# Attention and a mixture of experts on one core: x of the last two experts turned by DMA transposes of 16-bit planes, their routings let go earlier, and 34 idle matmuls for 12 behind the first gather

## The chip, the core and the metric

The kernel runs on one core of one Trainium2 chip. The core has five engines with queues of their own: TensorE (PE in the profile; its weight loads stand as PEld), VectorE (DVE), ScalarE (ACT), GpSimd (POOL) and SyncE (SP), which here only issues DMAs. The metric is the device time of one execution in microseconds (us), as the median of several. Profiles come from one profiled execution; their times count from the start of its span. L855 means line 855 of the kernel.

## What is computed

Attention with capped scores over 8 batches of 12 heads, 448 positions and 64 dimensions, and behind it a mixture of 8 experts, in float32:

```
scores = cap*tanh(q k^T/(8*cap));  attn = softmax(scores);  x = attn v      # x: 3584 tokens x 768
logits = x @ w_gate                                                        # 3584 x 8
# all 28672 logits in falling order: a token goes to an expert if it has none yet
# and the expert has fewer than cap = 3584/8 = 448 tokens
for e in range(8):
    h = relu(x[mask_e] @ w1[e])          # 448 x 768 @ 768 x 1024
    out[mask_e] = h @ w2[e]              # 448 x 1024 @ 1024 x 768
```

## The kernel before

The attention fills the first 335 us or so. Its last part, and the search that fills the first expert (routing 0), end at about 370 us. From there PE runs the experts one behind the other, in the order in which they filled; p counts them from 0 to 7.

**An expert.** Its 448 tokens' rows are fetched from the DRAM tensor xs by four indirect DMAs of POOL (`gather`, L782: rows 0-127, 128-255, 256-383, 384-447 of the expert, group j=0 to 3) into the tile xg. As the first product needs x with its 768 dimensions across partitions, x is turned: `xtr` (L798) turns one chunk c of 128 dimensions with four PE transposes, and `cutx` (L803, L804) reads them from PSUM and cuts them into a high part in PE's short float format and a low rest (xgh, xgl). Weights come in pieces by SP (`load1`, `load2`: w1r in four buffers, w2r in four) and are cut in the same way by ACT (L755) and POOL (L759) in `split1` and `split2`. `ffn1` computes h in 8 steps f of 18 matmuls of 448 columns (6 chunks times high-high, high-low, low-high): 144 matmuls. `ffn2` computes the output in 8 tiles u, of 24, 24, 24 and 16 matmuls of 384 columns, twice: 176 matmuls. Their results lie in psH, which has three buffers in PSUM; ACT evacuates each (L833 in ffn1, L861 and L864 in ffn2), with DVE behind it in ffn1 (L835). POOL scatters the output rows (L840).

**The order of the work.** For PE, ACT, DVE and POOL the program's order is the order of issue (manual_schedule); SP's order in this part is left to a planner. One matmul of ffn1 or ffn2 is one tick; an expert has 320. `tick` issues other work at set ticks: the next step of the routing generator, scatters, and the next expert's gather as soon as its tokens are known (L810). The routing of expert p+1 runs beside expert p: a search of three selections (not for the last expert), then `finalise`, which writes the expert's number (`ei`, L609) and token list (`idx`, L648). A hold in `phases0` (L678) lets finalise go at tick 145 of expert p's 320, the first of ffn2, for p+1 from 2 on. The turning of x for expert p+1 lies in tiles u=5, 6 and 7 of expert p's ffn2 (the table CP); two pieces of its weights are cut at u=5 and u=6. SP's loads for expert p+1 wait for ei and for free buffers.

**The start of the experts.** Behind routing 0 three pieces of w1 are loaded, the first gather is issued, and 12 idle matmuls (`warm(NW)`, L711; each stands in the profile as two records) keep PE at work. Then the steps of the next routing follow, whose first PE work (L477) waits for DVE, then `tx`, which turns four chunks as the four groups land, with four idle matmuls between two groups, and then the first matmul of ffn1. Further loads wait for the third group of the gather, by a copy of one value of it (tok).

Of the kernel before, what the change touches and what calls it, by code (L numbers as in the profile page):

```python
# [323 lines left out]


YL=[]
ACF=1
LF=1
TA=0
# [2 lines left out]
class Routing:  # L332
# [266 lines left out]
    def finalise(s,wp,L,update):  # L599
# [8 lines left out]
        ei=wp.tile([1,1],I32,name="ei",bufs=8)  # L608
        v.tensor_scalar(ei,s.e8s[0:1],-1.0,8.0,op0=ALU.mult,op1=ALU.add)  # L609
        s.ei=ei  # L610
        yield 8 if s.cur==1 else 12
        ps=s.psum()
        warm=(lambda n: s.warm(n)) if s.cur==0 else (lambda n: None)
        nc.tensor.matmul(ps[:112,0:2],s.lo,sc[:,:,NC-1],start=True,stop=False)
# [19 lines left out]
        ps=s.psum()  # L634
# [8 lines left out]
        ps=s.psum()  # L643
# [5 lines left out]
        s.results.append((idx,s.ei))  # L649
        yield 1  # L650
        if update:
          with s.tc.issue_after(mark.ins) if s.cur==0 else nullcontext():
            z=wp.tile([112,1],F32,name="zz")
            v.tensor_scalar(z,oi[:,0,0,0:1],0.0,None,op0=ALU.mult)
# [14 lines left out]
    def phases0(s,wp,L,turned):  # L669
        HA=[7,10]; HB=3  # L670
        for p in range(s.E):
            s.hA=HA[min(p,len(HA))-1] if p else 7; s.hB=HB; s.na=2 if p<9 else 1
            s.cur=p
            if p:
                s.propose(L,0,s.NC)
                yield 30
            yield from (s.search(wp,turned if p==0 else ()) if p<s.E-1 else s.last(wp))
            yield -((p-1)*320+145) if p>1 else 4  # L678
            yield from s.finalise(wp,L,p<s.E-1)


W1B=4; W2B=4
def ffn_all(nc, tc, ctx, rt, xs, w1, w2, out, ident, E, wp, deferred, xctx, gen):
# [11 lines left out]
    def units(n):  # L695
        for _ in range(n):
            if deferred: late.append(deferred.pop(0)())
    def posts():
        while late: late.pop(0)()
    N0=1; UN=[1,2,1,2,0,2,2,1,2,2,0,2,2,2,0,0]  # L700
    ctx.enter_context(tc.manual_schedule(engines={ET.PE,ET.Activation,ET.DVE,ET.Pool}))
    with tc.issue_after(rt.mark[0].ins):
        units(1)
    posts()
    m=0
    wu=[None]; end=[-99]
# [22 lines left out]
    def need(p):  # L729
        while len(res)<=p: step()  # L730
    ereg={}
    def expert(p):
        need(p)
        if p not in ereg: ereg[p]=nc.sync.value_load(res[p][1][0:1,0:1],min_val=0,max_val=E-1)
        return ereg[p]
    raw={}; spl={}; lp=[False]; tt=[False]
    gap=f2.tile([1,1],F32,name="gap")
    def load1(p,i,gate=None):
        if p>=E: return
        e=expert(p)  # L740
        t=ws.tile([128,DC,128],F32,name="w1r",bufs=W1B)
        if gate is not None: nc.gpsimd.tensor_copy(t[0:1,0,0:1],gate)
        nc.sync.dma_start(t,w1[bass.ds(e,1),:,i*128:i*128+128].rearrange("o (c p) f -> p (o c) f",p=128))
        raw[p,1,i]=t
# [31 lines left out]
    nc.gpsimd.memset(xgp[64:128,3*DM:],0.0)  # L776
    def gather(p):
        if p>=E or p in xgs: return
        need(p)
        t=xgs[p]=xgp  # L780
        for j,(o,n) in enumerate(TS):
            g=nc.gpsimd.indirect_dma_start(out=t[:n,j*DM:(j+1)*DM],out_offset=None,in_=xs,in_offset=bass.IndirectOffsetOnAxis(ap=res[p][0][:n,j:j+1],axis=0))  # L782
        return g
    def tx(p,n):
        newx(p)
        w=rt.psum()
        ps=[(ph.tile([128,512],F32,name="psH") if c>1 else pt.tile([128,512],F32,name="psX")) for c in range(n)]
        for j,(o,_) in enumerate(TS):
            for c in range(n): nc.tensor.transpose(ps[c][:,o:o+128],xgs[p][:,j*DM+c*128:j*DM+c*128+128],ident)
            if j<len(TS)-1: warm(WJ,w)  # L790
        for c in range(n): cutx(p,c,ps[c])
    def xtr(p,c):
        if p>=E or c is None: return
        newx(p)
        gather(p)
        ps=pt.tile([128,512],F32,name="psX")
        for j,(o,n) in enumerate(TS):
            nc.tensor.transpose(ps[:,o:o+128],xgs[p][:,j*DM+c*128:j*DM+c*128+128],ident)  # L798
        cutx(p,c,ps)
    def cutx(p,c,ps):  # L800
        h,l=xgT[p]
        src=ps[:,:C]
        nc.scalar.activation(h[:,c,:],src,AF.Copy)  # L803
        lo=nc.vector.tensor_tensor(l[:,c,:],src,h[:,c,:].bitcast(F32),op=ALU.subtract)  # L804
    pend=[]; cnt=[0]; cur=[0]; bc=[0]; BG=11
    def tick(n=1):
        cnt[0]+=n; bc[0]+=n; now[0]+=n
        if bc[0]>=BG:
            if pend: bc[0]=0; scatter(*pend.pop(0))
        if len(res)>cur[0]+1 and cur[0]+1 not in xgs: bc[0]=0; gather(cur[0]+1)  # L810
        if cnt[0]>=hint[0]:
            cnt[0]=0; step()
    hh={}
# [62 lines left out]
    step(); step()  # L876
    step()
# [5 lines left out]
    for p in range(E):  # L883
# [34 lines left out]

def full(nc,tc,q,k,v,cap,wg,w1,w2,out):
    with ExitStack() as ctx:  # L920
# [26 lines left out]
        ffn_all(nc,tc,ctx,r,xs,w1,w2,out,ident,8,wp,deferred,xctx,r.phases(wp,L1,turned))  # L947


_INS=["q","k","v","cap","moe_w_gate","moe_w1","moe_w2"]  # L950
# [24 lines left out]
```

## Time and profile before

| | us |
|---|---|
| median of 3 runs | 906.33 |
| lowest, highest | 905.64, 906.44 |
| the profiled execution | 906.85 |
| its span | 905.1 |

The 1.75 us between the profiled execution's time and its span lie outside of the instructions. The page of the profile lists the busy time of the engines. Views of the trace used below are the order of time of one engine (start, duration, engine, line, operation, tiles, count; in brackets the idle time before it and what ended it), groups of instructions by line, the stretches of time with the busy time and count of each engine, and the DMA issues with their time to landing.

### The profile page before, as it was taken

The numbers are of one execution on the slowest core, as the hardware profiler recorded it, in microseconds if no ns is written. First come the engines' busy times: TensorE is split into PE (matmuls) and PEld (weight loads), VectorE is DVE, ScalarE is ACT, GpSimd is POOL, SyncE is SP. The second block draws the span as 40 slices with busy tenths as digits, with TensorE's granted clock in tenths as the row PEclk, the third lists the DMA queues.
The fourth block names the chain that finished last, engine by engine and source line by source line (L and its number), as shares of the span: only waits on it lengthen the run. The fifth ranks groups of instructions, "written<-read, shape, count | busy, mean of one in ns | idle before, by whom it ended". The sixth has DMA issues, their size and how long they took to land.

```text
span 905.1 us, 17559 instructions
## 1 busy us (share of the span) xinstructions
PE 876.5 (97%) x6320; PEld 643.3 (71%) x6320; DVE 604.0 (67%) x2004; ACT 564.0 (62%) x844; POOL 349.9 (39%) x501
## 2 busy tenths in 40 slices
PE   6899999999999997799999999999999999999997
PEld 3333444444333345789989989989999999999997
DVE  3688988989888888766776776767767764231210
ACT  6998898889899948273582672762752752532521
POOL 8100000000000009482593492592682773754841
PEclk9999999999999999999999999999999999999999
DMA  8799999997994017741915616407407407416301
GB/s 117 113 136 140 128 171 173 139 164 120 198 175 72 1 58 246 248 157 45 313 45 171 196 36 226 157 19 236 150 18 253 149 3 251 149 55 236 112 10 53
DMA packets 291704, 123.09 MB, mean 136 GB/s; under 512 B 224768, under 2 KB 275712, under 8 KB 291104
## 3 DMA queue, kind: packets, MB, share of 16 engines
q1 hardware_dynamic: 285104, 99.70, 49.9%
q0 software_dynamic: 4656, 22.02, 6.8%
q8 instruction: 50, 0.82, 0.4%
q10 hardware_dynamic: 1856, 0.23, 0.2%
q14 instruction: 38, 0.31, 0.1%
HBM read 97.15 MB, written 24.77 MB: 135 GB/s over the span
## 4 chain that ended last, share of the span: by engine, by line
PE 72%; issue 12%; POOL 5%; DVE 5%; SPq 3%; DMA 1%; ACT 1%; POOLq 0%; ACTq 0%; DVEq 0%
PE psH L827 20%; PE psH L855 18%; PE psA L189 12%; PE psS L148 10%; PE psM L206 4%; SPq L92 2%; PE psS L153 2%; POOL w1l L759 2%; PE psX L798 2%; PE psM L37 1%; POOL out_dram L840 1%; POOL w2l L759 1%; DVE es L165 1%; POOL xg L782 1%; DVE cmpD L503 1%
## 5 line engine op out<-in xcount | busy, mean ns | idle before, releaser
L855 PE MATMUL psH<-w2h,hh 128*128 128x384 f32 x896 | 247.0, 342 | 0.0
L855 PE MATMUL psH<-w2l,hh 128*128 128x384 f32 x512 | 175.0, 342 | 0.0
L154 ACT ACTIVATE e<-psS 128x896 f32<-128x896 f32 x168 | 147.6, 909 | 31.3 <-PE psS L148 18.7
L855 PEld LDWEIGHTS psH<-w2h,hh 128*128 128x128 f32 x896 | 162.3, 189 | 0.2
L159 ACT ACTIVATE e<-e,bias 128x1792 f32<-128x1792 f32 (+2 forms) x74 | 147.3, 1991 | 2.0
L827 PE MATMUL psH<-xgh,w1h 128*128 128x448 f32 x384 | 143.4, 373 | 0.3 <-ACT xgh L803 0.3
L827 PE MATMUL psH<-xgh,w1l 128*128 128x448 f32 x384 | 141.6, 369 | 0.0
L827 PE MATMUL psH<-xgl,w1h 128*128 128x448 f32 x384 | 141.2, 368 | 0.0
L148 PE MATMUL psS<-tq,tk 64*64 64x448 f32 x1152 | 130.9, 548 | 7.4 <-DVE tq L133 3.4
L759 POOL TENSOR_TENSOR w1l<-w1r,w1h 128x768 fp32r<-128x768 f32 x62 | 114.2, 1843 | 28.6 <-ACT w1h L755 22.5
L189 PE MATMUL psA<-e,nv 64*64 64x448 f32 x1104 | 120.9, 541 | 1.2 <-DVE xT L199 1.2
L759 POOL TENSOR_TENSOR w2l<-w2r,w2h 128x768 fp32r<-128x768 f32 x64 | 118.1, 1846 | 9.0 <-ACT w2h L755 8.7
L459 POOL TENSOR_SCALAR r_Bt<-r_b 112x4 f16<-112x4 int32 x1 | 0.2, 199 | 303.7 <-DVE rin L243 303.7
L165 DVE TENSOR_TENSOR es<-es,e 64x896 f32<-64x896 f32 (+2 forms) x74 | 100.4, 1356 | 2.7 <-ACT e L159 1.3
L835 DVE SCALAR_TENSOR_TENSOR hh<-psH,hh 128x64 fp32r<-128x64 f32 (+1 forms) x128 | 44.1, 386 | 81.2 <-ACT hh L833 79.7
L861 ACT ACTIVATE on<-psH 128x384 f32<-128x384 f32 x48 | 23.6, 491 | 119.6 <-PE psH L855 119.6
L855 PEld LDWEIGHTS psH<-w2l,hh 128*128 128x128 f32 x512 | 96.5, 189 | 0.0
L148 PEld LDWEIGHTS psS<-tq,tk 64*64 64x64 f32 x1152 | 43.7, 133 | 73.9 <-issue 40.7
L189 PEld LDWEIGHTS psA<-e,nv 64*64 64x64 f32 x1104 | 46.5, 134 | 59.9 <-issue 50.5
L833 ACT ACTIVATE hh<-psH 128x448 fp32r<-128x448 f32 x64 | 34.8, 544 | 73.2 <-PE psH L827 61.1
L827 PEld LDWEIGHTS psH<-xgh,w1h 128*128 128x128 f32 x384 | 72.5, 189 | 5.9 <-ACT xgh L803 0.5
L827 PEld LDWEIGHTS psH<-xgh,w1l 128*128 128x128 f32 x384 | 72.3, 188 | 5.7
(334 smaller groups left out, 1320.6 us busy)
## 6 DMA issues: line engine op xcount, KB each, us to landing
w1r<-in_moe_w_dram SPq DMA_DIRECT2D x64, 384.0 KB, 3.9
w2r<-in_moe_w_dram SPq DMA_DIRECT2D x32, 768.0 KB, 8.0
k<-in_k_dram SPq DMA_DIRECT2D x92, 112.0 KB, 3.4
q<-in_q_dram SPq DMA_DIRECT2D x92, 112.0 KB, 4.0
nv<-in_v_dram SPq DMA_DIRECT2D x72, 128.0 KB, 3.9
xs<-xn SPq DMA_DIRECT2D x4, 1344.0 KB, 7.4
xs<-xn SPq DMA_DIRECT2D x4, 896.0 KB, 5.1
xd<-xT SPq DMA_DIRECT2D x2, 1344.0 KB, 7.0
```

The costliest lines, as they stand in the source:

```text
L148: for c in range(2): nc.tensor.matmul(ps[c*64:c*64+64,h,:S],tks[g,0][hp,o,u*128+c*64:u*128+c*64+64],tks[g,1][hp,o,:],start=True,stop=True)
L154: nc.scalar.activation(ev(g,r),ps[:,:,:S],AF.Tanh,scale=sr[0])
L159: act=lambda: nc.scalar.activation(e,e,AF.Exp,scale=sr[1],bias=bias)
L165: t=es_t[g]; add=lambda o,a,b: nc.vector.tensor_tensor(o,a,b,op=ALU.add)
L189: nc.tensor.matmul(avp[g,o][h*64:h*64+64,:S],lhs,rhs[hp,h,:],start=(j==0 and x==0),stop=j==3)
L206: nc.tensor.matmul(ps[g*32:g*32+32,:S],lhs,rhs,start=first,stop=last)
L759: (eng or nc.gpsimd).tensor_tensor(view(l),r,view(h).bitcast(F32),op=ALU.subtract)
L827: nc.tensor.matmul(ps[:,:C],a[:,c,:],b[:,c,:],start=(m==0),stop=(m==DC*3-1)); m+=1
L833: nc.scalar.activation(h[:,:C],ps[:,:C],AF.Relu)
L835: nc.vector.scalar_tensor_tensor(h[:,d:d+b-a],ps[:,a:b],0.0,h[:,a:b].bitcast(F32),op0=ALU.max,op1=ALU.subtract)
L855: nc.tensor.matmul(ps[:,:HD],h[:,f,a:a+128],spl[p,2,hf,f//2][w][:,f%2,:],start=(m==0),stop=(m==nm-1))
L861: if t<3: nc.scalar.activation(ons[p][0][:,t*DM+hf*HD:t*DM+hf*HD+HD],ps[:,:HD],AF.Copy)
```

## The change

For p from FT=6 on, PE no longer turns x. Instead, for each group j, ACT copies the gathered float32 rows, seen as 16-bit halves, into a tile pl with one plane of low and one of high halves, and its queue writes them to a DRAM tensor xz with the two planes of a token as neighbouring rows. When two groups are written, one DMA transpose of SP's queue turns 16-bit elements of [512, 768] or [384, 768] back into xg, where the two halves of a number come to lie side by side: x is turned, as float32. `cutt` then cuts it from SBUF, in four steps (two halves k of the tokens, three chunks each) at matmuls 8, 13, 18 and 23 of tile u=6. xg becomes two tiles, one for each k. `planes` of the groups follow the gather by 26, 36, 46 and 56 ticks.

For these two experts finalise is let go at tick 125 and 118 instead of 145 and waits 18 ticks instead of 12 for its first matmul; `early` issues the loads of three pieces of w1 and one of w2 as soon as ei is computed. SP's order is the program's from the start of the experts on, three blocks that asked the planner for an order are gone, and NW is 34 instead of 12.

```diff
+LK=(0,0,145,145,145,145,125,118); FT=6
...
+        if s.cur>=FT: s.early(s.cur,ei)
-        yield 8 if s.cur==1 else 12
+        yield 8 if s.cur==1 else 18 if s.cur>=FT else 12
...
-            yield -((p-1)*320+145) if p>1 else 4
+            yield -((p-1)*320+LK[p]) if p>1 else 4
...
-    ctx.enter_context(tc.manual_schedule(engines={ET.PE,ET.Activation,ET.DVE,ET.Pool}))
-    with tc.issue_after(rt.mark[0].ins):
-        units(1)
+    ctx.enter_context(tc.manual_schedule(engines={ET.PE,ET.Activation,ET.DVE,ET.Pool,ET.SP}))
+    units(1)
...
+    def early(p,ei):
+        ereg[p]=nc.sync.value_load(ei[0:1,0:1],min_val=0,max_val=E-1)
+        for i in range(3): load1(p,i)
+        load2(p,0)
+    rt.early=early
...
-    xgp=fp.tile([128,4*DM],F32,name="xg")
+    xgp=[fp.tile([128,2*DM],F32,name=f"xg{k}") for k in range(2)]
+    row=lambda j,n=128: xgp[j//2][:n,j%2*DM:(j%2+1)*DM]
...
+    TD=26; TJ=10; xq=[]
+    def planes(j):
+        o,n=TS[j]; k,r=divmod(j,2)
+        pl=fp.tile([128,2,DM],I16,name="pl",bufs=2)
+        nc.scalar.activation(pl[:n],row(j,n).bitcast(I16).rearrange("p (d h) -> p h d",h=2),AF.Copy)
+        nc.scalar.dma_start(xz[k][r*256:r*256+2*n].rearrange("(p h) d -> p h d",h=2),pl[:n])
+        if r:
+            n=o+n-2*128*k
+            nc.sync.dma_start_transpose(xgp[k][:,:DC*n].bitcast(I16).rearrange("p (c t) -> p c t",c=DC),xz[k])
+    def cutt(p,k,c0,c1):
+        newx(p)
+        o,n=((0,256),(256,192))[k]
+        h,l=(t[:,c0:c1,o:o+n] for t in xgT[p])
+        x=xgp[k][:,c0*n:c1*n].rearrange("p (c t) -> p c t",c=c1-c0)
+        nc.scalar.activation(h,x,AF.Copy)
+        nc.vector.tensor_tensor(l,x,h.bitcast(F32),op=ALU.subtract)
...
-        if len(res)>cur[0]+1 and cur[0]+1 not in xgs: bc[0]=0; gather(cur[0]+1)
+        if len(res)>cur[0]+1 and cur[0]+1 not in xgs:
+            bc[0]=0; n=cur[0]+1; gather(n)
+            if n>=FT:
+                xq.extend((now[0]+TD+TJ*j,lambda j=j: planes(j)) for j in range(4))
+        while xq and xq[0][0]<=now[0]: xq.pop(0)[1]()
...
-    WG=3; NW=12; WJ=4
+    WG=3; NW=34; WJ=4
     for i in range(WG): load1(0,i)
-    mk=gather(0)
-    with tc.issue_after(mk.ins):
-        tok=xgp[0:1,2*DM:2*DM+1]
-        for i in range(WG,W1B): load1(0,i,tok)
-        load2(0,0,tok)
-        load2(0,1,tok)
+    gather(0)
+    tok=xgp[1][0:1,0:1]
+    for i in range(WG,W1B): load1(0,i,tok)
+    load2(0,0,tok)
+    load2(0,1,tok)
     warm(NW)
...
-            if u==4: load1(p+1,0); load1(p+1,1)
-            if u==5: load1(p+1,2); load2(p+1,0)
+            if p+1<FT:
+                if u==4: load1(p+1,0); load1(p+1,1)
+                if u==5: load1(p+1,2); load2(p+1,0)
             if u==6: load1(p+1,3)
             if u==7: load2(p+1,1)
...
-            ffn2(p,u%4,u//4,(CL if p<1 else CP)[u],wk)
+            if p+1>=FT and not lastp:
+                for m,k,c in {6:[(8,0,0),(13,1,0),(18,0,3),(23,1,3)]}.get(u,()): wk[m]=wk.get(m,[])+[lambda k=k,c=c: cutt(p+1,k,c,c+3)]
+            ffn2(p,u%4,u//4,(CL if p<1 else CP)[u] if p+1<FT else [],wk)
...
+        xz=[dr.tile([n,768],I16,name=f"xz{i}") for i,n in enumerate((512,384))]
```

More of the change, by code (lines that the diff above doesn't have):

```diff
@@ L651, in finalise @@
         if update:
-          with s.tc.issue_after(mark.ins) if s.cur==0 else nullcontext():
+          if True:
             z=wp.tile([112,1],F32,name="zz")
@@ L677, in phases0, with ffn_all @@
             yield from (s.search(wp,turned if p==0 else ()) if p<s.E-1 else s.last(wp))
-            yield -((p-1)*320+145) if p>1 else 4
+            yield -((p-1)*320+LK[p]) if p>1 else 4
             yield from s.finalise(wp,L,p<s.E-1)
 W1B=4; W2B=4
-def ffn_all(nc, tc, ctx, rt, xs, w1, w2, out, ident, E, wp, deferred, xctx, gen):
+def ffn_all(nc, tc, ctx, rt, xs, xz, w1, w2, out, ident, E, wp, deferred, xctx, gen):
     C=448; DM=768; DC=6; DF=1024; FC=8; HD=384
@@ L732, in expert @@
     def expert(p):
+        if p in ereg: return ereg[p]
         need(p)
-        if p not in ereg: ereg[p]=nc.sync.value_load(res[p][1][0:1,0:1],min_val=0,max_val=E-1)
+        ereg[p]=nc.sync.value_load(res[p][1][0:1,0:1],min_val=0,max_val=E-1)
         return ereg[p]
@@ L774, in newx @@
         if p not in xgT: xgT[p]=(fp.tile([128,DC,C],F32R,name="xgh"),fp.tile([128,DC,C],F32R,name="xgl"))
-    xgp=fp.tile([128,4*DM],F32,name="xg")
-    nc.gpsimd.memset(xgp[64:128,3*DM:],0.0)
+    xgp=[fp.tile([128,2*DM],F32,name=f"xg{k}") for k in range(2)]
+    row=lambda j,n=128: xgp[j//2][:n,j%2*DM:(j%2+1)*DM]
+    nc.gpsimd.memset(xgp[1][64:128,DM:],0.0)
     def gather(p):
@@ L779, in gather @@
         need(p)
-        t=xgs[p]=xgp
+        xgs[p]=1
         for j,(o,n) in enumerate(TS):
-            g=nc.gpsimd.indirect_dma_start(out=t[:n,j*DM:(j+1)*DM],out_offset=None,in_=xs,in_offset=bass.IndirectOffsetOnAxis(ap=res[p][0][:n,j:j+1],axis=0))
+            g=nc.gpsimd.indirect_dma_start(out=row(j,n),out_offset=None,in_=xs,in_offset=bass.IndirectOffsetOnAxis(ap=res[p][0][:n,j:j+1],axis=0))
         return g
@@ L788, in tx @@
         for j,(o,_) in enumerate(TS):
-            for c in range(n): nc.tensor.transpose(ps[c][:,o:o+128],xgs[p][:,j*DM+c*128:j*DM+c*128+128],ident)
+            for c in range(n): nc.tensor.transpose(ps[c][:,o:o+128],row(j)[:,c*128:c*128+128],ident)
             if j<len(TS)-1: warm(WJ,w)
@@ L797, in xtr @@
         for j,(o,n) in enumerate(TS):
-            nc.tensor.transpose(ps[:,o:o+128],xgs[p][:,j*DM+c*128:j*DM+c*128+128],ident)
+            nc.tensor.transpose(ps[:,o:o+128],row(j)[:,c*128:c*128+128],ident)
         cutx(p,c,ps)
+    TD=26; TJ=10; xq=[]
[14 more added lines that the diff above has]
+        nc.vector.tensor_tensor(l,x,h.bitcast(F32),op=ALU.subtract)
     def cutx(p,c,ps):
@@ L946, in full @@
         deferred=[lambda f=f: f((px,xr)) for f in deferred]
-        ffn_all(nc,tc,ctx,r,xs,w1,w2,out,ident,8,wp,deferred,xctx,r.phases(wp,L1,turned))
+        ffn_all(nc,tc,ctx,r,xs,xz,w1,w2,out,ident,8,wp,deferred,xctx,r.phases(wp,L1,turned))
 _INS=["q","k","v","cap","moe_w_gate","moe_w1","moe_w2"]
```

## The prediction

> **What bounds the kernel now.** The page comes first, for the share of each engine.
>
> ```profile
> span 905.1 us, 17559 instructions
> PE 876.5 (97%) x6320; PEld 643.3 (71%) x6320; DVE 604.0 (67%) x2004; ACT 564.0 (62%) x844; POOL 349.9 (39%) x501
> ```
>
> PE is busy 97% of the span, but that is an average. The view by stretches, cut at the first matmul of an expert, says it of the stages that the change touches (columns: length, then busy time and count of PE, PEld, DVE, ACT, POOL, then PE's granted clock, DMA share, GB/s):
>
> ```profile
> 710.00:776.30 66.30, 66.30 (x375) 62.26 (x374) 37.39 (x168) 30.70 (x62) 38.57 (x43) 1.00 0.45 147
> 776.30:840.10 63.80, 63.80 (x353) 60.47 (x352) 14.48 (x41) 23.31 (x39) 37.39 (x41) 1.00 0.44 143
> ```
>
> These are the sixth and seventh experts (p=5 and 6), beside whose matmuls x of p=6 and 7 is gathered and turned. PE is never idle in either; ACT is idle for half of them, DVE for 29 us of the first. Whatever leaves PE here comes off the end, and a wait of PE is added to it in full. Second comes the order of time on PE around one turning of x (L798) in ffn2:
>
> ```profile
> 764.09 0.51 PE L855 MATMUL psH<-w2h,hh 128*128 128x384 f32 x2
> 764.44 0.34 PE L855 MATMUL psH<-w2l,hh 128*128 128x384 f32 x1
> 764.62 0.60 PE L798 MATMUL psX<-ident,xg 128*128 128x128 f32 x4
> 764.97 0.60 PE L855 MATMUL psH<-w2h,hh 128*128 128x384 f32 x2
> 765.40 0.34 PE L855 MATMUL psH<-w2l,hh 128*128 128x384 f32 x1
> ...
> 776.34 0.36 PE L827 MATMUL psH<-xgh,w1h 128*128 128x448 f32 x1
> ```
>
> Starts count, not durations, since matmuls overlap. Two L855 matmuls take 0.35 us from start to start (764.09 to 764.44); the four transposes take 0.35 (764.62 to 764.97), and the two behind them 0.43 (764.97 to 765.40). One chunk of x costs PE 0.35+0.08 = 0.43 us.
>
> **Part 1: transposes taken off PE.** Six chunks for each of two experts go: 12 x 0.43 = **5.2 us less**, all on the path. The six evacuations of each (L803, L804) become four pairs of cutt, of about the same elements, on engines with idle time.
>
> **Part 2: 34 idle matmuls for 12.** The order of time on PE behind the routing of the first expert, its idle matmuls as a group, POOL's last gather, the landing of the four gathers, and a stretch with its granted clock:
>
> ```profile
> 369.96 2.92 PE L711 MATMUL psX<-ident 128*128 128x128 f32 x24
> 375.45 0.27 PE L477 MATMUL psR<-r_id,r_VA 112*128 112x112 f16 x2 [2.56 <-DVE r_VA L452]
> 375.77 0.41 PE L789 MATMUL psX<-ident,xg 128*128 128x128 f32 x2
> 376.01 0.38 PE L789 MATMUL psH<-ident,xg 128*128 128x128 f32 x2
> 376.23 1.27 PE L711 MATMUL psR<-ident 128*128 128x128 f32 x8
> ...
> 380.54 1.06 PE L711 MATMUL psR<-ident 128*128 128x128 f32 x8
> 381.43 0.38 PE L789 MATMUL psX<-ident,xg 128*128 128x128 f32 x2
> ```
>
> ```profile
> L711 PE MATMUL psX<-ident 128*128 128x128 f32 x96 | 12.5, 280 | 0.0
> ```
>
> ```profile
> 375.05 1.14 POOL L782 DMA_INDIRECT xg<-xs,idx  x1 [0.30 <-issue]
> ```
>
> ```profile
> DMA to landing us min/median/max: 4.4/4.4/4.6
> ```
>
> ```profile
> 377.00:378.00 1.00, 1.00 (x7) 1.00 (x6) 1.00 (x2) 0.00 (x0) 0.00 (x0) 0.50 0.61 203
> ```
>
> Twelve idle matmuls are 24 records, 2.92 us for all; the last is 0.28 long (L711's mean), so they start (2.92-0.28)/23 = 0.115 us apart. 34 are 68: L477 starts at 369.96+68x0.115 = 377.8 instead of 375.45, and the first transposes at 378.1. The last gather lands at 375.05+4.4 = 379.5, so from then on PE waits for none. At full clock a round is 0.46 (four transposes, 375.77 to 376.23) and 0.89 (eight records, 380.54 to 381.43): the fourth round starts at 378.1+3x1.35 = 382.15, against 381.43 before, where three rounds ran partly at a clock of 0.50. **0.75 us more**, which the PE behind it passes on to the end. If the half clock stayed, it would be the whole 2.35 us (rival 4). DVE's split of w1 (L759) waits for L477 and still ends ahead of L803.
>
> Of this the Trainium skill, "TensorE: Matmul & The Clock Gate", section "Why this matters for your kernels", says that a gap in PE's work of more than about 3 us brings the half clock. The gap here is 2.56 us, and the trace shows the half clock behind it, so here row and rule differ. By the rule this gap wouldn't be the cause, longer idling wouldn't cure it, and the sum would be that of rival 4.
>
> **Part 3: the chain that takes the transposes' place.** For p=6, in the clock of the trace of before. The rows, of DVE, SP and POOL in order of time, of two groups on ACT, of the DMA issues (KB each, us to landing; the gathers are those of this stretch), of the 40 slices (tenths that the DMA engines are busy, and GB/s), and of a stretch at full rate:
>
> ```profile
> 739.12 0.08 DVE L575 DVE_READ_ACCUMULATOR sx<-wt,wB,r_e8c 112x1 f32 x1
> ...
> 744.48 0.12 DVE L609 TENSOR_SCALAR ei<-e8s 1x1 int32<-1x1 f32 x1
> ```
>
> ```profile
> 745.41 1.63 SPq L743 DMA_DIRECT2D w1r<-in_moe_w_dram  x3
> ```
>
> ```profile
> 750.65 0.98 POOL L782 DMA_INDIRECT xg<-xs,idx  x1 [8.57 <-DVE zz L654]
> 751.93 1.20 POOL L782 DMA_INDIRECT xg<-xs,idx  x1 [0.31 <-issue]
> ```
>
> ```profile
> L159 ACT ACTIVATE e<-e,bias 128x1792 f32<-128x1792 f32 (+2 forms) x74 | 147.3, 1991 | 2.0
> L755 ACT ACTIVATE w1h<-w1r 128x768 fp32r<-128x768 f32 x64 | 53.5, 836 | 9.4 <-DMA w1r<-in_moe_w_dram 9.4
> ```
>
> ```profile
> w1r<-in_moe_w_dram SPq DMA_DIRECT2D x64, 384.0 KB, 3.9
> ...
> wgs<-in_moe_w_gate_dram SPq DMA_DIRECT2D x6, 4.0 KB, 2.0
> ```
>
> ```profile
> xg<-xs,idx POOLq DMA_INDIRECT x4, 7.7
> ```
>
> ```profile
> DMA 8799999997994017741915616407407407416301
> GB/s 117 113 136 140 128 171 173 139 164 120 198 175 72 1 58 246 248 157 45 313 45 171 196 36 226 157 19 236 150 18 253 149 3 251 149 55 236 112 10 53
> ```
>
> ```profile
> 384.00:386.00 2.00, 2.00 (x13) 1.82 (x13) 1.41 (x4) 1.58 (x4) 1.54 (x1) 1.00 1.00 398
> ```
>
> The routing is let go at tick 125 of ffn1 instead of 145, but DVE ends the search (sx) only at 739.2, so ei comes at about 740.0 instead of 744.5, and SP's loads start at about 741 instead of 745.4. They are 3x384+768 KB = 1.9 MB; at 398 GB/s they are through by 747. With 18 ticks instead of 12 before its matmul, results come at tick 125+18+18+8 = 169 instead of 183: 14 ticks of ffn2, of 0.174 us (0.35 for two), so the gather starts at about 750.65-2.4 = 748.2, and its four at 1.3 us from each other land at 752.6 to 756.5, by the 4.4 us of the first gather, now that no weights run beside it.
>
> Each planes() is an ACT copy of 1536 elements a partition: by 836 ns for 768 and 1991 for 1792, 1.7 us, and 0.5 for the DMA issue on ACT's queue (three took SP 1.63). The write of 384 KB takes 4.0 (w1r's loads of that size 3.9). pl has two buffers, so the third planes waits for the first write:
>
> planes 0: 752.6 to 754.3, written 758.8. Planes 1: 754.8 to 756.5, written 761.0. Planes 2: 758.8 to 760.5, issued 761.0. Behind it on ACT stands the evacuation of the third tile (0.5), then planes 3: 761.5 to 763.2, issued 763.7, written 767.2 (half the size, 3.5).
>
> Both transposes are SP's: 786 KB at 761.0 and 590 KB at 767.2. Before shows no such DMA. Its bounds: a fixed 2.0 us, as the 4 KB of wgs, and 398 GB/s, the full rate of large packets, or 136 GB/s, the rate of the attention's slices in which the engines are 9 tenths busy with small packets. The second lands at 770.7 or at 773.5. I take the middle, 772, since the rate lies between those of large and small packets.
>
> When is it late? Without the transposes, ffn1 of p=6 starts at 776.34-6x0.43 = 773.75. The first half of cutt for k=1 is 576 elements on ACT (0.65) and as many on DVE (0.7), so landing by 772.4 costs nothing, and at 773.5 it costs 1.1 us. For p=7 the routing is let go 7 ticks sooner (118), which is 1.3 us more slack: nothing, even at 136 GB/s. I charge **0.4 us more**, in a range of 0 to 1.1.
>
> Other waits it could bring: SP's next loads (w1 of f=3, w2 of i=1) queue behind the transposes, at about 768 instead of 748. They land by 775 (1.9 MB at 398 GB/s and 2.0) and are first split in f=1, after 773.75+18x0.174 = 776.9, for use in f=3: hidden. DVE's second part of finalise now stands ahead of the evacuation of f=7 (L835); the first tile of ffn2 needs that only at its 23rd matmul, 22x0.174 = 3.8 us after it starts, and DVE idles for 29 of the 66 us: hidden, and worth about a microsecond if not. SP's own order elsewhere is nearly that of before: SP already ran ahead of the tiles, and the gate on w1r follows the same third gather. The split of xg in two tiles costs nothing.
>
> One rule speaks against the change. The Trainium skill, "VectorE: DVE Perf Modes", section "The three transpose paths", gives 1309 ns to a 128x128 block of 16-bit data by DMA, where TensorE takes 390 ns. Taken one behind the other, the 24+18 blocks would be an estimate of 55 us per expert from that page. No run of before can show it; rival 3 has the mechanism.
>
> **Sum.** -5.2+0.75+0.4 = -4.05 us. The profiled execution took 906.85 us, of which 905.1 are its span, so it would be 902.8; against the median of 906.33, half a microsecond lower: **902.3 us**.
>
> **The rivals.**
> 1. The chain is one to two microseconds later per expert. Planes 2 holds the evacuation of the third tile on ACT, which the sixth tile needs (psH has three buffers): it begins 64 matmuls of 0.174 and six chunks of 0.43 ahead of 776.34, at 762.6, one microsecond after my 761.5. For: the gathers of p=6 before took 7.7 us, not 4.4. Against: the weights then ran beside them. 2 to 4 us come back: 904.3 to 906.3.
> 2. Slower. The same place, ACT's queue in front of psH and of cutt, with slow transposes: every microsecond of landing after 772.4 is one of PE for p=6 (773.7 for p=7), and 772.4 plus 2.9 is where p=6 and 7 together have eaten the 4.45 of parts 1 and 2. It needs 590 KB to take over 6 us, below 100 GB/s; the slowest slices with busy engines moved 113. Time: 908.2 to 914.
> 3. The transposes go block by block, each a round trip of 2.0 us: 84 us from 761.0, 72 late, twice: about 1050.
> 4. The half clock of 377 stays: -5.2+2.35+0.4 = 903.9.
>
> **How the numbers follow.** Forecast 0.60 (901.4 to 903.2), rival 1 0.20, rival 2 0.14, rival 3 0.02, rival 4 0.04. 0.2% of 906.33 is 1.8 us, about what a measurement of this kernel can tell from no change; the limits are 904.5 and 908.1. Faster: 0.60+0.04 and 0.08 of rival 1; same: the other 0.12; slower: 0.16. The range goes from 901.0 (no lateness, part 2 at 0.5, 0.4 of scatter) to 908.0, leaving out rivals 2 and 3.
>
> **What would show it.** No L798 in ffn2 of p=5 and 6, and these stretches 2.6 us shorter with PE still never idle; PE's clock at 1.00 from 370 to 383, and the first L827 0.75 us later; DMA landings of the transposes at about 5 us each; no wait of L827 on xgh or of L855 on ACT. PE waits at the sixth tile or at the first L827 of p=6 or 7 would make the prediction wrong, and so would a first L827 no later than before.

## The result, and the profile after

| | before | after |
|---|---|---|
| median (us) | 906.38 (6 runs, 905.64 to 906.69) | 900.43 (6 runs, 899.97 to 902.15) |
| the profiled execution, its span | 906.85, 905.1 | 900.64, 898.9 |

The ratio of the times is 0.9937, with a 95% interval of 0.9925 to 0.995: 5.95 us less. Forecast were 4.05 less (902.3 us), and the range began at 901.0, so the result lies 0.6 us below its lower end.

The page of the kernel after, for the share of each engine:

```profile
span 898.9 us, 17579 instructions
PE 874.1 (97%) x6316; PEld 641.9 (71%) x6316; DVE 609.8 (68%) x2000; ACT 573.9 (64%) x848; POOL 348.7 (39%) x501
```

The view by stretches of the kernel after, cut at the first matmul of ffn1 and ffn2 of p=5, 6 and 7 (columns as in the prediction):

```profile
712.47:742.89 30.42, 30.42 (x157) 26.95 (x157) 21.90 (x110) 20.51 (x43) 26.82 (x29) 1.00 0.18 54
742.89:774.00 31.11, 31.11 (x183) 30.79 (x182) 15.24 (x50) 13.88 (x18) 11.08 (x11) 1.00 0.85 248
774.00:803.35 29.35, 29.35 (x148) 27.15 (x148) 10.48 (x23) 14.57 (x22) 27.05 (x31) 1.00 0.43 139
803.35:834.45 31.10, 31.10 (x183) 30.78 (x181) 8.66 (x17) 13.77 (x18) 10.69 (x11) 1.00 0.84 251
834.45:863.64 29.19, 29.19 (x146) 27.05 (x145) 5.38 (x15) 14.57 (x22) 27.25 (x33) 1.00 0.41 137
```

The same cuts in the kernel before:

```profile
712.07:742.32 30.25, 30.25 (x154) 26.84 (x154) 21.12 (x104) 20.51 (x43) 26.86 (x29) 1.00 0.17 52
742.32:776.33 34.01, 34.01 (x208) 33.41 (x207) 14.59 (x56) 8.68 (x16) 11.29 (x12) 1.00 0.67 219
776.33:806.09 29.76, 29.76 (x146) 27.04 (x146) 5.99 (x16) 14.61 (x23) 26.66 (x29) 1.00 0.18 55
806.09:840.12 34.03, 34.03 (x208) 33.42 (x207) 8.49 (x25) 8.69 (x16) 10.73 (x12) 1.00 0.66 220
840.12:869.87 29.75, 29.75 (x146) 27.03 (x146) 5.99 (x16) 14.60 (x23) 27.01 (x31) 1.00 0.18 54
```

PE is busy for all of each stretch in both kernels, so the lengths are what counts. The two ffn2 are 2.90 and 2.93 us shorter: 24 records of transposes and one other are gone from each (208 to 183). That was foreseen. Not foreseen are the two ffn1 behind them: 29.35 and 29.19 for 29.76 and 29.75, though their 144 matmuls and their granted clock of 1.00 are the same. In the last one, with no record more or fewer, a matmul takes 29.19/144 = 202.7 ns from start to start instead of 206.6.

The order of time on PE at the start of the experts, after:

```profile
370.00 7.84 PE L712 MATMUL psX<-ident 128*128 128x128 f32 x68
377.67 0.26 PE L478 MATMUL psR<-r_id,r_VA 112*128 112x112 f16 x2
377.77 0.45 PE L797 MATMUL psX<-ident,xg 128*128 128x128 f32 x2
...
381.83 0.38 PE L797 MATMUL psX<-ident,xg 128*128 128x128 f32 x2
382.05 0.38 PE L797 MATMUL psH<-ident,xg 128*128 128x128 f32 x2
382.74 0.47 PE L855 MATMUL psH<-xgh,w1h 128*128 128x448 f32 x1 [0.31 <-ACT xgh L827]
```

PE's gap of 2.56 us is gone; 0.31 is left ahead of the first ffn1, as before. The fourth round of transposes starts at 381.83 instead of 381.43, 0.40 later.

The new chain, as ACT and SP show it for p=6:

```profile
752.56 1.49 ACT L812 ACTIVATE pl<-xg 128x1536 int16<-128x1536 int16 x1
...
757.85 1.48 ACT L812 ACTIVATE pl<-xg 128x1536 int16<-128x1536 int16 x1 [1.47 <-DMA xz<-pl]
...
759.75 0.49 ACT L889 ACTIVATE on<-psH 128x384 f32<-128x384 f32 x1 [0.42 <-ACT pl L812]
760.13 1.47 ACT L812 ACTIVATE pl<-xg 64x1536 int16<-64x1536 int16 x1
...
768.38 0.83 ACT L822 ACTIVATE xgh<-xg 128x768 fp32r<-128x768 f32 x1
770.48 1.99 ACT L822 ACTIVATE xgh<-xg 128x576 fp32r<-128x576 f32 x3 [1.27 <-DMA xg<-xz]
```

```profile
758.93 9.51 SPq L816 DMA_TRANSPOSE xg<-xz  x2
768.69 0.39 SPq L745 DMA_DIRECT2D w1r<-in_moe_w_dram  x1
```

The third copy waits 1.47 us for a buffer and the evacuation L889 stands behind it, as forecast. The second of the two DMA transposes is issued from 765.60 on, and its data is there by 770.48, 4.9 us later. ACT waits for the second transpose until 770.48; PE, whose ffn1 starts at 774.00, waits for nothing.

From before to after, by the starts of the stages:

| step | forecast | in the two traces |
|---|---|---|
| up to the first ffn1 (part 2) | +0.75 | +0.40 |
| 12 chunks of transposes (part 1) | -5.2 | about -5.5 |
| lateness of the chain (part 3) | +0.4 | 0 |
| pace of ffn1, p=6 and 7 | no term | -1.13 |
| sum | -4.05 | -6.23 (spans: -6.2) |

The two ffn2 lose 2.90+2.93 and the three ffn1 gain 0.17, -0.41 and -0.56. A pair of small matmuls of finalise (L616) has moved from each of these ffn2 into the ffn1 ahead of it, at about 0.17 each. So the chunks are 5.83 less 0.34, and the pace is 0.41+0.17+0.56 = 1.14.

### The profile page after: what moved, and what is told of

The parts are those of the page before. It is cut to its first block, busy times and chain, and to the rows that moved or that the text cites. A ratio compares the mean times of both kernels' runs of the same rounds, so it can differ in the third digit from the quotient of the medians.

```text
span 898.9 us, 17579 instructions
## 1 busy us (share of the span) xinstructions
PE 874.1 (97%) x6316; PEld 641.9 (71%) x6316; DVE 609.8 (68%) x2000; ACT 573.9 (64%) x848; POOL 348.7 (39%) x501
## 4 chain that ended last, share of the span: by engine, by line
PE 40%; issue 11%; POOL 5%; POOLq 0%; DMA 0%; DVE 0%; ACT 0%
PE psH L855 20%; PE psH L883 18%; POOL w1l L761 2%; PE psX L806 2%; POOL out_dram L868 1%; POOL w2l L761 1%; POOL xg L790 1%; DMA w1r<-in_moe_w_dram 0%; POOL gap L759 0%; PE psR L638 0%; PE psR L508 0%; POOLq L927 0%; PE psV L478 0%; POOLq L1001 0%; DVE cmpD L504 0%
## 5 line engine op out<-in xcount | busy, mean ns | idle before, releaser
L889 ACT ACTIVATE on<-psH 128x384 f32<-128x384 f32 x48 | 23.5, 490 | 109.8 <-PE psH L883 92.1
L863 DVE SCALAR_TENSOR_TENSOR hh<-psH,hh 128x64 fp32r<-128x64 f32 (+1 forms) x128 | 44.0, 385 | 71.0 <-ACT hh L861 69.4
```

Source lines behind the costliest of these rows:

```text
L863: nc.vector.scalar_tensor_tensor(h[:,d:d+b-a],ps[:,a:b],0.0,h[:,a:b].bitcast(F32),op0=ALU.max,op1=ALU.subtract)
L889: if t<3: nc.scalar.activation(ons[p][0][:,t*DM+hf*HD:t*DM+hf*HD+HD],ps[:,:HD],AF.Copy)
```

## The experiments

Before is about 906.3 in every set (906.22 to 906.58), with executions from 904.55 to 907.84; ratios are to it.

### What the gain hangs on

**The change without planes.** The change with x of all experts turned on PE and all routings let go at tick 145; SP's order, xg in two tiles and 34 idle matmuls stay.

```diff
-LK=(0,0,145,145,145,145,125,118); FT=6
+LK=(0,0,145,145,145,145,145,145); FT=8
```

> The changed kernel without its main part: no planes and no early loads, x of all experts turned on PE, all routings let go at tick 145; SP's order, the split of xg and the 34 idle matmuls stay. Theory: all that was gained hangs on the transposes taken off PE, so this is before plus the 0.4 us of the idle matmuls: about 906.8 us, with ffn1 of the last two experts at 29.75 us and their matmuls 206.7 ns apart. Rival: SP's order or the split of xg carry part of the gain that the forecast lacked (1.1 us in ffn1 of the last two experts): about 905.6, with those matmuls 202.6 ns apart.

Measured: 906.98 us (906.61 to 907.47), ratio 1.001 (1.0 to 1.0019). All of the gain came with the planes and the earlier routing; the next run parts the two.

**The early routing alone.** As that, but with the routings and first loads of p=6 and 7 as early as in the change.

```diff
-LK=(0,0,145,145,145,145,125,118); FT=6
+LK=(0,0,145,145,145,145,125,118); FT=8; EF=6
...
-        if s.cur>=FT: s.early(s.cur,ei)
-        yield 8 if s.cur==1 else 18 if s.cur>=FT else 12
+        if s.cur>=EF: s.early(s.cur,ei)
+        yield 8 if s.cur==1 else 18 if s.cur>=EF else 12
...
-            if p+1<FT:
+            if p+1<EF:
                 if u==4: load1(p+1,0); load1(p+1,1)
```

> The changed kernel with x of p=6 and 7 turned on PE again, but with their routings and first loads let go as early as in the change (ticks 125 and 118, 18 ticks to the matmul pair L616), 34 idle matmuls. It tells what of the change set the fast pace of ffn1 of p=6 and 7 (202.7 ns for 206.6), now that neither a chunk of transposes ahead of ffn1 nor a bare interruption does. If the pair L616, moved from the head of ffn2 into ffn1, sets it: pace 202.7 and about 905.8 us. Rival, that the absence of the transposes from the rest of ffn2 (or where the tiles lie) sets it: pace 206.6 and about 907.0 us.

Measured: 906.85 us, ratio 1.0009 (1.0 to 1.0018). ffn1 of p=7 takes 29.75, so the moved pair isn't what sets the pace, and letting go earlier gives nothing by itself: the gain hangs on the planes.

### The 34 idle matmuls

**Twelve as before**, all else as in the change.

```diff
-    WG=3; NW=34; WJ=4
+    WG=3; NW=12; WJ=4
```

> The changed kernel with 12 idle matmuls as before. Theory: the 34 cost 0.4 us net (first matmul of ffn1 at 382.74 against 382.34 before), so this gives about 900.0 us, with the stretch at half clock back between 377 and 380 and the first matmul at 382.3. Rival: the 34 help or are needed by the rest of the change (loads, SP's order): 901 or more.

Measured: 899.22 us (898.85 to 900.21, 4 runs), ratio 0.9927 (0.9911 to 0.9944). PE in that profile:

```profile
369.90 2.92 PE L712 MATMUL psX<-ident 128*128 128x128 f32 x24
375.39 0.27 PE L478 MATMUL psR<-r_id,r_VA 112*128 112x112 f16 x2 [2.57 <-DVE r_VA L453]
375.71 0.41 PE L797 MATMUL psX<-ident,xg 128*128 128x128 f32 x2
```

and the stretch behind the gap:

```profile
377.00:378.00 1.00, 1.00 (x12) 1.00 (x11) 1.00 (x2) 0.00 (x0) 0.00 (x0) 1.00 0.83 281
```

The gap is the one of before, but the granted clock is 1.00, where before it was 0.50. So the half clock behind this gap isn't sure to come. A later run with 12 had it again:

```profile
377.00:378.00 1.00, 1.00 (x7) 1.00 (x6) 0.48 (x1) 0.00 (x0) 0.42 (x3) 0.50 0.06 12
```

From the start of the idle matmuls to the first matmul of ffn1, six profiles with 34 show 12.74 us each. Nine profiles with 12 show 12.3 to 12.4 in six (clock 0.50), 12.1 in one, and 11.1 and 11.5 in the two at 1.00. So 34 cost 0.4 us where the half clock would have come, and up to 1.7 where not; they never gain.

**Twenty-four**, which end just as L478 can start:

```diff
-    WG=3; NW=34; WJ=4
+    WG=3; NW=24; WJ=4
```

> The changed kernel with 24 idle matmuls behind the first gather instead of 34. Theory: the idle matmuls cost what they hold PE beyond the release of L478 by DVE (375.45 in the trace of before) and pay by keeping PE's clock at 1.00. 24 are 48 records of 0.115 us, so they end at about 375.5, just at that release; four rounds of 1.33 us at full clock then put the last round at about 379.6, where the last group of the gather lands (375.08+4.4 = 379.5), and the first matmul of ffn1 at about 380.6 instead of 382.74: about 898.3 us, faster than both kernels. Rival: the gather, the split of w1 or the clock holds PE there anyway, and nothing is gained: 900.4. Second rival: the clock falls to half all the same: about 900.

Measured: 903.98 us (903.01 to 905.24), ratio 0.9974 (0.9964 to 0.9983). The first ffn1 matmul came at 381.21, 1.5 us earlier, as expected, yet the whole is 3.5 us slower. PE lost it far behind, in ffn1 of p=6:

```profile
799.93 0.36 PE L855 MATMUL psH<-xgh,w1h 128*128 128x448 f32 x1
802.67 0.16 PE L616 MATMUL psR<-scan,r_lo 112*112 112x2 f16 x1 [2.38 <-DVE ei L610]
...
804.16 0.58 PE L855 MATMUL psH<-xgh,w1h 128*128 128x448 f32 x1
804.53 0.58 PE L855 MATMUL psH<-xgl,w1h 128*128 128x448 f32 x1
```

PE waits 2.38 us for the routing of p=7, and then its matmuls are 0.37 apart instead of 0.2, at half the granted clock, as behind the gap of before:

```profile
803.60:804.60 1.00, 1.00 (x5) 0.88 (x4) 0.95 (x5) 0.00 (x0) 0.00 (x0) 0.50 0.06 18
```

The next views, DVE and POOL of that kernel, say why:

```profile
795.83 6.16 DVE L604 TENSOR_SCALAR gt<-qq,wB 112x32 f32<-112x32 f32 x1
```

```profile
794.64 1.84 POOL L761 TENSOR_TENSOR w1l<-w1r,w1h 128x768 fp32r<-128x768 f32 x1
...
798.32 1.84 POOL L761 TENSOR_TENSOR w2l<-w2r,w2h 128x768 fp32r<-128x768 f32 x1
...
800.16 1.79 POOL L761 TENSOR_TENSOR w2l<-w2r,w2h 128x768 fp32r<-128x768 f32 x1
```

L604 works on 32 elements a partition and takes 0.23 us elsewhere. Here it ends at the moment when POOL's unbroken series of cuts ends, at 801.95. The changed kernel has the same in a milder form:

```profile
797.27 3.18 DVE L604 TENSOR_SCALAR gt<-qq,wB 112x32 f32<-112x32 f32 x1
...
801.83 1.15 DVE L620 SCALAR_TENSOR_TENSOR pG<-scan,psR,gteq 112x32 f32<-112x32 f16 x1
```

```profile
798.57 1.84 POOL L761 TENSOR_TENSOR w2l<-w2r,w2h 128x768 fp32r<-128x768 f32 x1
800.36 0.12 POOL L759 MEMSET gap<- 1x1 f32 x1
801.10 1.84 POOL L761 TENSOR_TENSOR w2l<-w2r,w2h 128x768 fp32r<-128x768 f32 x1 [0.61 <-ACT w2h L757]
```

There POOL has to wait 0.61 us for ACT at 800.4, L604 gets through, and finalise's 18 ticks hide its 3.18 us. L620, 0.26 us elsewhere in this trace, takes 1.15 and ends with the cut that starts at 801.10. With 24 idle matmuls PE was 1.5 us earlier there and POOL's series only 0.25 (798.32 for 798.57), so POOL no longer had to wait for ACT, and the gap was gone. In the kernel before, L603 (the same step) started at 807.47, behind the series, and took 0.23.

The Trainium skill, "SBUF — State Buffer", section "SBUF: two separate sides", states that DVE and GpSimd share one pair of SBUF ports as an exclusive lock, held for a whole instruction, and that the loser blocks; of DVE's operations it names those in a two-port mode and those with two inputs in SBUF. That L604 is one of these no run shows. The rows agree with such a lock, and they go further than one instruction: a DVE step of 0.23 us is held for as long as POOL's instructions follow each other without a gap, in the run with 24 through four cuts.

**One cut moved from POOL to DVE**, with 24, 12 and 34 idle matmuls, all on one chip.

```diff
-            if f+2<FC and (p,1,f+2) not in spl: work[3]=[lambda: split1(p,f+2)]
+            if f+2<FC and (p,1,f+2) not in spl: work[3]=[lambda: split1(p,f+2,nc.vector if p==6 and f==0 else None)]
```

> The changed kernel with 24 idle matmuls, as in the run with 903.98 us, and one of POOL's 16 cuts of p=6 (the w1 of its third tile, taken in f=0) moved to DVE at a time when DVE idles. Theory, that DVE's first step of finalise (L604) can't start while POOL's cuts follow each other without a gap, and that PE's wait at L616 and the slow matmuls behind it are only that: POOL is 1.84 us less behind, its series has a gap before 799, L604 takes at most 3.2 us instead of 6.16, ffn1 of p=6 goes from 32.7 to 29.3, and the time is 899.0 to 899.6 us. Rival, that L604 was late for another reason: 903.5 to 904 us again.

> The same with 12 idle matmuls. No wait at L616 in either case; it stands beside the next on one chip, so that the two differ in the idle matmuls alone. If a half clock behind the 2.56 us gap comes only in some executions: 899.0 to 899.6 us, first ffn1 matmul at 381.0 or, with the half clock, 382.3.

> The same with 34 idle matmuls, as in the change. By the term of the prediction (0.75 us more than 12): 0.75 above the run with 12. If the half clock mostly stays away with 12: 1.2 to 1.6 us above it, 900.2 to 900.6. The move of the cut itself should do nothing here, since L604's 3.2 us were hidden.

| idle matmuls | us | ratio | L604 (us) |
|---|---|---|---|
| 24 | 899.84 (898.79 to 900.65) | 0.9933 (0.992 to 0.9947) | 2.88 |
| 12 | 899.33 (898.45 to 900.42) | 0.9929 (0.9916 to 0.9943) | 0.38 |
| 34 | 900.07 (899.51 to 900.86) | 0.9939 (0.9926 to 0.9953) | 0.35 |

With 24 the wait at L616 is gone and with it 4.1 us (3.4 between the spans of the two traces):

```profile
796.45 2.88 DVE L604 TENSOR_SCALAR gt<-qq,wB 112x32 f32<-112x32 f32 x1
```

```profile
799.23 0.13 POOL L759 MEMSET gap<- 1x1 f32 x1
800.27 1.83 POOL L761 TENSOR_TENSOR w2l<-w2r,w2h 128x768 fp32r<-128x768 f32 x1 [0.91 <-ACT w2h L757]
```

POOL's gap is back, now 0.91 us, and L604 ends in it. So the series of cuts was the cause. The time came out 0.2 us above what was expected: the first two matmuls of ffn1 of p=6 are 0.68 us apart here, as the last cut of x (L823) is late by that much for a PE that is earlier. Between 12 and 34 the medians differ by 0.74, within the scatter of either; the traces (0.4 to 1.7) say the same more sharply.

### How much slack the chain has

**The planes 20 ticks later.**

```diff
-    TD=26; TJ=10; xq=[]
+    TD=46; TJ=10; xq=[]
```

> The changed kernel with the four planes steps 20 ticks later (46 instead of 26 behind the gather). 20 ticks of ffn2 are 3.5 us, so the second transpose of p=6 would land at about 774.0 instead of 770.5. If the slack is as the trace of the changed kernel has it (harmless up to 772.4), PE waits about 1.6 us ahead of ffn1 of p=6 and a little less for p=7: 903.0 to 903.6 us, with a wait of L855 on xgh or of its first matmuls on ACT or DVE. Rival, that the chain is held by the landing of the gathers and the first write and not by the ticks: 900.4 us.

Measured: 906.28 us (904.36 to 907.77), ratio 0.9999 (0.999 to 1.0009): the whole gain is lost. PE at the head of ffn1 of p=6:

```profile
773.33 0.34 PE L883 MATMUL psH<-w2l,hh 128*128 128x384 f32 x1
...
773.97 0.48 PE L855 MATMUL psH<-xgh,w1h 128*128 128x448 f32 x1 [0.30 <-ACT xgh L822]
774.76 0.47 PE L855 MATMUL psH<-xgl,w1h 128*128 128x448 f32 x1 [0.32 <-DVE xgl L823]
```

and all waits of PE from 740 to 840, of the same kernel:

```profile
PE psR L616 <- DVE ei L610: 2.5, 1, 2.5
PE psH L855 <- DVE xgl L823: 0.3, 1, 0.3
PE psH L855 <- ACT xgh L822: 0.3, 1, 0.3
```

The cut of the second half starts at 773.24 instead of 770.48, 0.84 past the prediction's limit of 772.4, and costs about 1.05 us (0.64 and 0.79 between starts, where 0.18 and 0.2 are normal); ahead of and in ffn1 of p=7 it is 1.4. So the lateness is some 2.5 us, close to the 2.6 to 3.2 of the theory, though p=7 lost more than p=6 and not less. The larger part, 4.2 us, is the wait at L616 with its half clock once more: L604 took 6.23 us. Neither theory had that in it.

**p=5 by planes too**, with 12 idle matmuls.

```diff
-LK=(0,0,145,145,145,145,125,118); FT=6
+LK=(0,0,145,145,145,125,125,118); FT=5
```

> The changed kernel with 12 idle matmuls behind the first gather as before, and with the turning by planes for p=5 too (routing of p=5 let go at tick 125). Theory: the six chunks of p=5 (2.64 us) and some 0.3 for the finalise matmuls leave PE in ffn2 of p=4: ffn2 of p=4 at 32.2 instead of 35.1, 899.2 - 2.6 = 896.6 us. Rival: beside ffn2 of p=4 the search for p=5 still runs on DVE and ACT, and the chain is late or the routing is: PE waits ahead of ffn1 of p=5, 899 to 902 us.

Measured: 905.64 us (902.05 to 910.6), ratio 0.9994 (0.9976 to 1.0012). In ffn2 of p=4 ACT still runs the search, and ACT's order is fixed:

```profile
691.53 1.49 ACT L812 ACTIVATE pl<-xg 128x1536 int16<-128x1536 int16 x1 [1.10 <-DMA xz<-pl]
...
695.97 0.51 ACT L501 ACTIVATE cmpA<-r_VAt,r_H8A 128x252 bf16<-128x252 f16 x1 [0.62 <-ACT pl L812]
```

and PE's waits for it:

```profile
697.25 0.17 PE L508 MATMUL psR<-r_ce,r_bo 128*128 128x8 bf16 x1 [3.06 <-ACT cmpA L501]
714.35 0.18 PE L508 MATMUL psR<-r_ce,r_bo 128*128 128x8 bf16 x1 [2.30 <-ACT xgh L822]
```

The search's counts (L501) queue behind the copies and behind cutt, PE waits for them, and ffn2 of p=4 takes 40.82 us instead of 32.2. The rival was right, and worse than it said. A part is not the search's: L604 took 6.23 us in this trace too, and with the wait at L616 ffn1 of p=6 takes 32.56 us instead of 29.35. The change stops at the experts whose ffn2 has no search beside it.

### What sets the pace of ffn1

In p=2 to 5 ffn1 runs at 202.7 ns between the small matmuls of the search in both kernels. In p=2 its first six intervals are 206.7, and the first small matmul turns it to 202.7. The ffn1 of p=6 and 7 have no search beside them. So the first idea was that an interruption sets the pace.

**A bare interruption**, in the kernel before:

```diff
+            if p>5 and f==0: work[7]=[lambda: nc.tensor.matmul(rt.psum()[:,:8],rt.bo,rt.cd8[0],start=True,stop=True)]
             ffn1(p,f,work)
```

> The kernel before with one tiny matmul more (8 columns, result unused) behind the seventh matmul of ffn1 of p=6 and p=7; the transposes stay on PE. Theory of the pace: PE's stream of ffn1 has two paces, 206.7 and 202.6 ns a matmul; behind a chunk of transposes it enters the slow one and stays there until something stands between two matmuls, as the routing's small matmuls do in p=2 to 5. Then the tiny one costs 0.12 us and the 137 matmuls behind it gain 4.1 ns each: ffn1 of p=6 and 7 falls from 29.75 to about 29.3 us, and the time by 0.9 us to about 905.5. Rival: the pace comes from how x was brought in (DMA and SBUF instead of PSUM, other traffic of DMA, ACT or DVE): it stays at 206.7 ns, and the time is 0.2 us longer, about 906.6.

Measured: 906.89 us, ratio 1.0005 (0.9996 to 1.0015); the pace stays 206.6 behind it. The idea falls.

**A chunk of idle transposes** four matmuls ahead of ffn1, in the kernel after:

```diff
+            if p+1>=FT and not lastp and u==7:
+                def turn(z):
+                    for j in range(4): nc.tensor.transpose(z[:,j*128:j*128+128],ident,ident)
+                wk[12]=[lambda: turn(pt.tile([128,512],F32,name="psX"))]
```

> The changed kernel with one chunk of idle transposes (four 128x128 blocks of the identity) put back 4 matmuls ahead of ffn1 of p=6 and 7, where the kernel before had its sixth chunk. Theory that a chunk of transposes close ahead of ffn1 sets the pace of its 144 matmuls: pace 206.6 ns, each expert 0.44 + 0.57 us more, so 900.4 + 2.0 = 902.4 us, ffn1 of p=6 and 7 at 29.9. Rival, that the short wait at the head of ffn1 in the changed kernel sets the fast pace: pace stays 202.7, only 2 x 0.44 more, 901.3 us.

Measured: 901.25 us, ratio 0.9948 (0.9933 to 0.9962). The pace stays 202.7, so a chunk there isn't it; the 0.8 us are two chunks.

**A short wait**, in the kernel before:

```diff
+            if p>5 and f==0:
+                def wait():
+                    z=rt.psum(); cw=wp.tile([128,8],F32,name="cw",bufs=2); z2=rt.psum()
+                    nc.tensor.matmul(z[:,:8],rt.bo,rt.cd8[0],start=True,stop=True)
+                    nc.vector.tensor_scalar(cw,z[:,:8],0.0,None,op0=ALU.mult)
+                    nc.tensor.transpose(z2[:8,:128],cw,ident)
+                work[7]=[wait]
             ffn1(p,f,work)
```

> The kernel before, with a short real wait in the stream of ffn1 of p=6 and 7: behind its 7th matmul a matmul of 8 columns, a DVE copy of its result, and a transpose of that copy, for which PE has to wait some 0.3 to 0.6 us. If a short wait moves PE to the fast pace: 206.6 becomes 202.7 ns for the 137 matmuls that follow, 0.53 us less for 0.4 to 0.7 more per expert, about 906.4 us, with pace 202.7 in both. Rival, that the pace is set otherwise: pace 206.6, 907.2 us.

Measured: 906.53 us, ratio 0.9999 (0.999 to 1.0008). The pace was 202.7, but from the first matmul on, ahead of the wait: something else in this kernel had moved it. What sorts all these traces is the last interval of ffn2, from its last matmul's start to the first of ffn1. In the trace's nanoseconds it is 182 in before, 181 or 182 with the bare interruption, 180 and 182 with the early routing alone (206.6 behind them), and 177 in after, 171 with the chunk, 177 or 178 with the wait (202.7). Three more kernels, all of them before with one edit, test this: an idle matmul of 8 columns behind the 14th matmul of the last tile of ffn2, the same behind the 8th, and a tile that nothing reads.

```diff
+            if p in (5,6) and u==7: wk={14:[lambda: nc.tensor.matmul(rt.psum()[:,:8],rt.bo,rt.cd8[0],start=True,stop=True)]}
             ffn2(p,u%4,u//4,(CL if p<1 else CP)[u],wk)
```

```diff
+            if p in (5,6) and u==7: wk={8:[lambda: nc.tensor.matmul(rt.psum()[:,:8],rt.bo,rt.cd8[0],start=True,stop=True)]}
```

```diff
     gap=f2.tile([1,1],F32,name="gap")
+    cw=wp.tile([128,8],F32,name="cw",bufs=2); nc.gpsimd.memset(cw,0.0)
```

> The kernel before, with one idle matmul of 8 columns in ffn2 of p=5 and 6, behind the 14th of the last tile's 16 matmuls, that is behind the last chunk of transposes and two matmuls ahead of ffn1. Theory, that the pace of ffn1 is the phase in which PE's stream enters it: the last interval of ffn2 changes from 181 to some other length below 179, ffn1 of p=6 and 7 run at 202.7 ns, 0.57 less each for 0.12 more, 905.3 us. Rival, that the transposes in ffn2 (all six chunks) set it whatever follows them: pace 206.6, 906.6 us.

> The same idle matmul behind the 8th of the last tile's matmuls, ahead of the last chunk of transposes. By the phase theory either pace can come, and the last interval ahead of ffn1 foretells it (180 to 182 ns with 206.6, 170 to 178 with 202.7); if the last chunk puts PE into one phase whatever came before it: 181 and 206.6, 906.6 us.

> The kernel before with one small tile more that nothing reads, so that other tiles lie elsewhere in SBUF, and no other edit. In the run with the short wait the pace was 202.7 from the entry of ffn1 on, ahead of the wait itself, and such a tile was in that kernel. If the place of the tiles sets the phase: 202.7, last interval 177, about 905.2 us. If not: 206.6, 181, 906.3 us.

| edit of before | last interval (ns), p=6 and 7 | ffn1 (us) | time (us) | ratio |
|---|---|---|---|---|
| idle matmul behind the 14th | 179, 180 | 29.75 | 906.13 | 0.9998 (0.9989 to 1.0007) |
| idle matmul behind the 8th | 171, 171 | 29.19 | 904.91 | 0.9986 (0.9978 to 0.9995) |
| unused tile | 178, 178 | 29.19 | 905.22 | 0.9989 (0.998 to 0.9998) |

The second of them, in the stretch from the first to the last of its 144 matmuls of p=6:

```profile
776.12:805.31 29.19, 29.19 (x144) 26.86 (x144) 1.00 0.18 55
```

It has all six chunks of transposes, the routing and the queues of before, and one matmul more, and it runs ffn1 as the changed kernel does; its time is 1.4 us lower (0.5 to 2.0 by the interval). With the unused tile it is 1.05 lower, where two stages at the other pace make 1.12. So the fast pace needs neither the planes nor the missing transposes: the place of one idle matmul decides it, or a tile that nothing reads.

Here this is called a phase: PE's stream of weight loads and matmuls enters ffn1 in one of a few alignments and keeps it. The bare interruption in p=6 and 7 didn't move it, the first small matmul in p=2 did. For p=6 and 7, in every trace here in which PE didn't wait at the entry, 171 to 178 ns went with 202.7 and 179 to 182 with 206.6; where it waited there, 202.7 followed. The interval is a sign at this one place and no rule. The edit behind the 14th was expected to bring 202.7 and didn't, its 179 lay between the two ranges set down before, and p=2 of the kernel before enters with 171 ns and runs at 206.7. What the alignment is inside of PE, and whether it is one of time or of the place of the tiles, the traces don't show, and it stays open.

## Why the prediction was right, and where it failed

**The bound** was right. PE is still busy for all of the stages concerned, and what left it came off the end.

**Part 1** was right, and a little small: 12 chunks gave 5.5 us instead of 5.2, as a chunk costs the intervals next to it a few ns more (up to 178 instead of 174 in the trace of before). The ffn2 of the early routing alone (33.82) and of the change (31.11) give 2.71/6 = 0.45 a chunk, where the prediction had 0.43.

**Part 2** had the right sign at nearly twice the size: the traces show +0.40 for +0.75. It took over the 0.32 us from L477 to the first transposes, which 12 idle matmuls show with and without the half clock (375.39 to 375.71 without); 2.3 us later it is 0.10 (377.67 to 377.77), which is 0.22 of the 0.35 that it was off; L477 came at 377.67 instead of 377.8. In all six profiles with 34 the clock is 1.00 from 375 to 383. The prediction also took the half clock behind the gap as given. In two of nine profiles with 12 it didn't come, and there 34 cost 1.3 and 1.7.

**Part 3** was right in its order and places. The gather starts at 748.59 (748.2), the third copy and the evacuation behind it stand at 757.85 and 759.75, and cutt of the second half starts at 770.48, just below the bounds (770.7 to 773.5). The copies took 1.48 instead of 1.7. The charge of 0.4 for lateness was not needed. With 20 ticks more the limit of 772.4 proved good to a few tenths.

**The rivals.** Rival 1's place is real: the evacuation of the third tile does stand behind the third copy (759.75), but it ends at 760.24, 2.7 us before the sixth tile (762.90) wants its buffer. Rivals 2 and 3 fell with the transposes: both are done 11.6 us after the first was issued (758.93 to 770.48), less than the 55 us that the prediction had estimated from the 1309 ns a block of the Trainium skill, "VectorE: DVE Perf Modes", section "The three transpose paths". Rival 4 fell, as the clock is 1.00 from 370 to 383.

**The step that failed** is that the sum had no term for the stages behind ffn2. It took ffn1 of p=6 and 7 to be the same 144 matmuls at the same price. They ran 4 ns faster each, 1.13 us in all, more than half of the 1.9 us by which the median was missed. The change doesn't bring that by what it takes away: before, with all its transposes and one idle matmul or one unused tile more, has it too. That the changed kernel came to the fast pace is luck. At the old pace it would have taken some 901.6 us, which is within the range. With this term the forecast would have been 901.2 us; the rest is what parts 1, 2 and 3 were off.

**What was missed and did no harm**: the earlier routing moves finalise's DVE steps from behind POOL's series of cuts into it. The prediction asked what queues behind a waiting instruction, but not which engine holds up an instruction that waits for no semaphore. In the changed kernel 0.61 us of idle POOL is all that stands between 900 and 904 us, and three edits closed it: 24 idle matmuls, the planes 20 ticks later, and p=5 by planes.

No variant here is clearly faster than the change. The one with 12 idle matmuls (899.22; with the moved cut 899.33) is lowest in the median and beats before clearly, but the interval of its ratio overlaps that of the change.

## What to carry to other kernels

Read stage lengths and counts side by side before and after, also where the edit isn't: a stage with the same instructions can change its pace, and a gain of 0.1% may be nothing but such a phase, so test it with an edit that does nothing. When a small DVE step is moved, look at what POOL does at that time, not only at semaphores; POOL's cuts in an unbroken series hold it until the next gap. Transposes by DMA are worth it where the engines that prepare them are idle, which here were the ffn2 with no search beside them, of p=5 and 6.

## What the runs showed of the hardware that wasn't expected

- A DVE step of 0.23 us took 3.18, 6.16 and 6.23 us beside POOL's two-input subtractions in a row, and ended with the series each time. L863, which reads one input from PSUM, was never held: none of its 128 in the changed kernel is over 0.55 us. L620, with two inputs in SBUF and a third in PSUM, was (1.15 us).
- The same 144 matmuls take 29.75 or 29.19 us at a granted clock of 1.00, as PE enters them: one idle matmul or one unused tile more elsewhere changes it.
- The same gap of 2.57 us was followed by a spell at a clock of 0.50 in seven profiles with 12 idle matmuls, and by none in two (mean clock from 375 to 383: 0.79 in six, 0.81 in one, 1.00 in two). The Trainium skill, "TensorE: Matmul & The Clock Gate", section "What's actually happening", describes a free-running activity window of 3413 ns and lets the half clock come after at least one idle window. The gap here is shorter than that and brought it in seven of nine; what decides it, no run here tests.
